# Matmuls of a gated layer listed ahead of their gate operations, and one group's exponentials listed directly behind its logarithms

## Chip, cores and metric

The kernel runs on one core of one Trainium2 chip. The metric is device microseconds (us) of one launch; less is better. TensorE (PE) multiplies matrices, VectorE (DVE) and ScalarE (ACT) work element by element, GpSimd (POOL) and SyncE (SP) issue transfers here. PEld is TensorE's loading of the stationary operand.

## What is computed

The reference has two blocks: a gated recurrence over 768 steps for 4 batches of 8 heads of width 48, and behind it a dense layer with a cosine gate.

```python
mag = np.sqrt(a_re * a_re + a_im * a_im)
scale = np.minimum(mag, 0.999) / (mag + 1e-06)
a_re_n, a_im_n = (a_re * scale, a_im * scale)
for t in range(S):
    new_re = ar * S_re - ai * S_im
    new_im = ar * S_im + ai * S_re
    kv = np.einsum('bhd,bhe->bhde', k[:, :, t], v[:, :, t])
    S_re, S_im = (new_re + kv, new_im)
    y[:, :, t] = np.einsum('bhd,bhde->bhe', q[:, :, t], S_re)
...
h = x @ w_in          # x: 3072 x 384, w_in: 384 x 2048
g = h * np.cos(h)
return (g @ w_out).astype(np.float32)
```

The attention inputs are float32. The two layer weights arrive as float64 and are turned into float32 on the chip.

## The kernel before

The 3072 rows are 24 chunks of 128 steps, worked on in 12 groups of two chunks (G = 2). In place of the recurrence, each chunk uses prefix sums. The logarithm of the decay's size and the angle of the decay are summed along the steps by a matmul with a triangular matrix; keys and queries are multiplied by the exponential of the one sum and the cosine and sine of the other; then a causal product of queries and keys gives the chunk's part, and a carried state the rest. The steps of one group g are:

- `logs(g)`, which calls `g_log`: squares, Ln and Exp on ACT with six DVE operations in between (tiles `lg`, `mag`, `rs`, `tan`), and then the load of the next group's `re` and `im`.
- `p_powers(g, i)`: matmuls of the sums (PSUM tile `lgs`) and two Exp on ACT for each chunk (`P`, in the buffer `lg`, and `Q`).
- `g_angle(g)`: one Arctan on ACT, in place in `tan`. `g_carry(g)` does nothing for groups 0 and 1.
- `p_even` and `p_apply`: three and two DVE operations on P, Q, k and q; `p_even` also issues the transfers `row` and `end` on SP.
- `phases(g)`, which calls `g_phase`: matmuls of the angles (PSUM tile `phs`), a cast on ACT and a subtraction on DVE for each chunk.
- `keys(g)`: `g_trig` (two Sin on ACT, one DVE operation) and `g_stack` (four DVE products, tiles `ks` and `qs`). For group 1, `turned` transposes them on PE (tile `tp`, copied to `kT` and `qT`).
- `chunks(g)`: causal products (`sc`), state (`sp`), output (`yp`), and at the end `f_xt`, which carries the result through memory into `xT`, the layer's input. Group 0 does this in its own way, by `f_rows` and `f_columns`.
- `first(g)`: eight calls of `mm1`. Each multiplies `xT` with one of eight parts of `w_in` into one PSUM bank (`hp`), takes Sin and Square of it on ACT (`gate`, `junk`) and multiplies on DVE (`gate`). `second(g, i)` multiplies the gates with `w_out` (`op`).

The weights come in 16 parts, 0 to 7 of `w_in` (`into`) and 8 to 15 of `w_out` (`back`), through four buffers `raw`. POOL issues the transfer of a part when a buffer is free. `convert` makes floats of a part: a TENSOR_SCALAR, a SCALAR_TENSOR_TENSOR and a CUSTOM_DVE on DVE, and one ACTIVATE on ACT between them (`raw`). The CUSTOM_DVE frees the buffer. The text calls these conversion 0 to 15. The first `RAW` = 4 of them are listed earlier.

The order comes from three things. The program order is a list that `weave` merges from several parts, each spread evenly over a stretch of the list. All matmuls, all table functions of ACT (`special`: Ln, Exp, Sin, Arctan) and all POOL transfers are chained and keep that order on their engine. The other operations of DVE, ACT and SP are set in a fixed order for each engine at build time, by their place in the list and by when the build reckons them ready. On the chip each engine then goes through its queue in order. Ln and Exp are in one table set of ACT and Arctan and Sin in another; `preload` lists a table load (line L699) at each change between them.

PSUM has eight banks: five of the pool `pa` (tag `a`), and three of `pm`, two with the tag `m` and one with the tag `acc`. An `hp` tile keeps its bank until its DVE product has read it.

Around the change the list before is: `logs(1)`, conversion 4, load of group 2's `re` and `im`, conversion 5, tile 0, conversion 6, tile 1, conversion 7, tiles 2 and 3, the two `p_powers(1)`, conversion 8, `g_angle(1)`, `p_even` and `p_apply`, load of group 2's `k` and `q`, tile 4, conversion 9, phase 0, tile 5, phase 1, conversion 10, `g_trig(1)`, tile 6, `g_stack(1)`, conversion 11, tile 7. "Tile" is one `mm1(0, jp)` with its matmuls and gate operations. Then a second `weave` has conversions 12 to 15, `second(0, 0)`, the transposes of group 1, `logs(2)`, `chunks(1)` and `prods(2)`. A third has `second(0, 1)`, `phases(2)`, `keys(2)` and `first(1)`, and from there the groups follow each other alike.

Of the kernel before, what the change touches and what calls it, by code (L numbers as in the profile page):

```python
# [11 lines left out]
F32 = mybir.dt.float32  # L12
# [475 lines left out]
def fast_path(ctx, tc, q, k, v, a_re, a_im, moe_w_in, moe_w_out, out, least, odd, wide):  # L488
# [9 lines left out]
    C = 128  # L498
    NCH = S // C
    G = 2  # L500
# [20 lines left out]
    pa = ctx.enter_context(tc.tile_pool(name="pa", bufs=5, space=PSUM))  # L521
    pm = ctx.enter_context(tc.tile_pool(name="pm", bufs=3, space=PSUM))
# [20 lines left out]
    X = [dict() for _ in range(NG)]  # L543
# [6 lines left out]
    def load(g, names, i=None, put=nc.sync.dma_start):  # L550
        for name in names:
            ap = {"re": a_re, "im": a_im, "q": q, "k": k, "v": v}[name]
            if name not in X[g]:
                X[g][name] = ld.tile([C, G, H, D], F32, tag=name, name=name,
                                     bufs=2 if name == "v" else 1)
            b, c = divmod(g * G + (i or 0), NCH)
            one, n = i or 0, G if i is None else 1
            steps = ap[b].rearrange("h (c p) d -> p c h d", p=C)[:, ds(c, n)]
            tile_ = X[g][name][:, ds(one, n)]
            parts = [(0, C, 0)]  # L560
            if name in ("re", "im") and g >= PEG:

                parts = [(0, C - 16, 1), (C - 16, C - 1, 1)]
                put(out=tile_[C - 1:C], in_=steps[0:1])
            for i_ in range(n):
                for lo, hi, by in parts:
                    put(out=tile_[lo:hi, i_], in_=steps[lo + by:hi + by, i_])
# [18 lines left out]
    RAW = stage["bufs"]  # L586
# [96 lines left out]
    def matmul(out, **kw):  # L683
        chain(nc.tensor.matmul(out, **kw), "tensor")  # L684
# [16 lines left out]
    def special(func, **kw):  # L701
        preload(tables[func])
        chain(nc.scalar.activation(func=func, **kw))  # L703
# [4 lines left out]
    def temp(tag, bufs=1):  # L708
        return gt.tile([C, G * DM], F32, tag=tag, name=tag, bufs=bufs)
# [5 lines left out]
    def cut(t, i, n):  # L715
        return (flat(t) if len(t.shape) == 4 else t)[:, ds(i * DM, n * DM)]
# [59 lines left out]
    def summed_up(ps, g, i, name, ones):  # L776

        if g < PEG:
            matmul(ps, lhsT=ones, rhs=cut(X[g][name], i, 1), start=True, stop=True)
            return  # L780
        chunks_ = range(i + 1) if name == "tan" else [i]
        terms = [(half, c) for half in ("hi", "lo") for c in chunks_]
        for half, c in terms:
            matmul(ps, lhsT=exact if c == i else alls, rhs=cut(X[g][half], c, 1),
                   start=((half, c) == terms[0]), stop=((half, c) == terms[-1]))

    def p_powers(g, i):

        x = X[g]
        if i == 0:  # L790
            x["P"], x["Q"] = x["lg"], temp("Q")
            x["row"] = rows_d.tile([G * DM], F32, tag="row", name="row")
            x["end"] = ft.tile([D2, G * H], F32, tag="end", name="end")
        ps = pa.tile([C, DM], F32, tag="a", name="lgs")
        summed_up(ps, g, i, "lg", sums[0])
        special(out=cut(x["P"], i, 1), in_=ps, func=AF.Exp)
        special(out=cut(x["Q"], i, 1), in_=ps, func=AF.Exp, scale=-1.0)
# [35 lines left out]
    def g_angle(g, i, n):  # L833

        at = cut(X[g]["tan"], i, n)
        special(out=at, in_=at, func=AF.Arctan)
# [172 lines left out]
            out=xt.rearrange("p c g t -> p c (g t)"),  # L1009
            in_=moved.rearrange("p s d t -> (p s d) t").rearrange("(c r) t -> r c t", r=C))  # L1010

    def mm1(g, jp):
        x = X[g]
        third = len(x.setdefault("gate", {})) % 3 == 2
        ps = pm.tile([C, 2, G * C], F32, tag="acc" if third else "m", name="hp",
                     bufs=1 if third else 2)
        for ji in range(2):
            for dc in range(ND):
                matmul(ps[:, ji], lhsT=w_in[:, jp, dc, ts(ji, C)],
                       rhs=x["xT"][:, dc].rearrange("p g t -> p (g t)"),  # L1020
                       start=(dc == 0), stop=(dc == ND - 1))
        gate = msb.tile([C, 2, G * C], F32, tag="gate", name="gate", bufs=8)
        junk = msb.tile([C, 2, G * C], BF16, tag="junk", name="junk", bufs=1)
        special(out=gate, in_=ps, func=AF.Sin, scale=1.0 / in_scale, bias=half_pi_b)
        scalar.activation(out=junk, in_=ps, func=AF.Square, scale=1.0 / in_scale,
                          accum_out=wide[:, ds(g * (NJ // 2) + jp, 1)])
        gated = vector.tensor_tensor(out=gate, in0=ps, in1=gate, op=ALU.mult)
        x.setdefault("gated", gated)
        x["gate"][jp] = gate

    def mm2(g, i, j0, nj):
        if j0 == 0:
# [104 lines left out]
    def weave(*parts):  # L1137

        items = []
        for p, (part, lo, hi) in enumerate(parts):  # L1140
            part = list(part)
            items += [(lo + (hi - lo) * (i + 0.5) / len(part), p, t)
                      for i, t in enumerate(part)]
        for _, _, t in sorted(items, key=lambda x: x[:2]):
            t()
# [4 lines left out]
    def keys(g):  # L1150

        if not 0 <= g < NG:
            return
        for i, n in spans(g):
            yield lambda i=i, n=n: g_trig(g, i, n)
            yield lambda i=i, n=n: (g_stack(g, i, n), p_end(g, i, n))
            for name in "kT", "qT":
                if g >= PEG:
                    yield lambda i=i, n=n, name=name: f_transpose(g, i, n, name)
# [4 lines left out]
    def prods(g):  # L1164
        if not 0 <= g < NG:
            return
        for i in range(G):
            yield lambda i=i: p_powers(g, i)
        yield lambda: g_angle(g, 0, G)
        yield lambda: g_carry(g)  # L1170
        yield lambda: (p_even(g, 0, G), p_apply(g, 0, G))

    def logs(g):
        yield from each(g_log, g)
        if 0 <= g and g + 1 < NG:
            yield lambda: load(g + 1, ("re", "im"))

    def phases(g):
        return [lambda i=i: g_phase(g, i) for i in range(G)] if 0 <= g < NG else []
# [11 lines left out]
    def first(g):  # L1191
        order = range(NJ // 2) if g < PLAIN else (0, 4, 1, 5, 2, 6, 3, 7)
        return [lambda jp=jp: mm1(g, jp) for jp in order]
# [4 lines left out]
    def convert(parts):  # L1198
        return [lambda dst=dst, src=src: weight(dst, src)() for dst, src in parts]
# [12 lines left out]
    into, back = weight_parts()  # L1212
# [35 lines left out]
    for t in (turned(0, 0, "kT") + turned(0, 0, "qT") + early[:1]  # L1248
# [5 lines left out]
              + [lambda: next(one, None), lambda: next(two, None),  # L1254
                             lambda: load(2, ("v",))]):
        t()
    weave((logs(1), 0.0, 0.1), (convert(into[RAW:]), 0.0, 0.5),
          (first(0), 0.2, 1.0), (prods(1), 0.55, 0.58), ([lambda: load(2, ("k", "q"))], 0.58, 0.6),
          (phases(1), 0.7, 0.8), (keys(1), 0.8, 0.9), (convert(back[:4]), 0.5, 1.0))
    over = [t for i in range(G) for name in ("kT", "qT") for t in turned(1, i, name)]  # L1260
    weave((convert(back[4:]), 0.0, 0.3), (second(0, 0), 0.0, 0.65), (over, 0.2, 0.6),
          (logs(2), 0.3, 0.31), (chunks(1), 0.7, 1.0), (prods(2), 0.85, 0.87))
# [89 lines left out]
```

## Time and profile before

| | before |
|---|---|
| median of 3 runs | 677.03 us (676.07 to 678.66) |
| span of the profiled execution | 677.3 us, 0.3 us above that median; the profile gives no other time for that execution |
| busy: PE, PEld, DVE, ACT, POOL | 647.8, 580.3, 490.3, 396.4, 28.5 us |
| ACT table loads | 26, 33.4 us |
| mean granted TensorE clock | 0.985 |

Busy times are of the whole span. The stretch that the change touches is about 48 to 123 us. A row of the timeline has start, duration, engine, line, operation, output <- inputs, shapes, count, and in brackets the idle time before it with what ended it. Line L684 is the helper that lists every matmul, L703 that of ACT's table functions, and L673 that of DVE's and ACT's other operations, so operations are told apart by tile names. A float32 matmul of the program shows as two MATMUL records; a tile `hp` has 12. Matmul rows of one kind are pipelined, so the time from one start to the next is used for their cost, not the printed length of a row.

### The profile page before, as it was taken

The page shows a single profiled execution, that of the slowest core. Times are in us where ns is not written, and L with a number is a line of the kernel's source. Part 1 is how long each engine was busy: PE and PEld are TensorE (multiplying, and loading weights), DVE is VectorE, ACT ScalarE, POOL GpSimd, SP SyncE. Part 2 cuts the span into 40 slices and gives each one's busy share as a digit, 9 for nine tenths or more (in the row PEclk, how much of TensorE's full clock was granted, in tenths as well). Part 3 has the DMA queues.
Part 4 walks back from the last instruction along what each step waited for, and adds up shares of the span by engine and source line. Part 5 has one row for each costly group of instructions (what it writes and reads, how often), then busy time and mean ns, then how long its engine had stood idle before and what let it go on. Part 6 is the DMA issues. An engine that isn't in the chain of part 4 may idle for free.

```text
span 677.3 us, 10771 instructions
## 1 busy us (share of the span) xinstructions
PE 647.8 (96%) x4080; PEld 580.3 (86%) x4080; DVE 490.3 (72%) x792; ACT 396.4 (59%) x730; POOL 28.5 (4%) x47
## 2 busy tenths in 40 slices
PE   5788889999999999999999999999999999999995
PEld 5686657886799999999999999989999989999895
DVE  4879888759868778868768778868768769762251
ACT  5869775475466467367467467467367467432330
POOL 2011100000000000000000000000000000000000
PEclk8979899999999999999999999999999999999998
DMA  9778623923743864764864864854864753363000
GB/s 244 176 234 224 173 72 81 227 66 69 213 92 63 219 137 116 210 142 109 224 140 118 210 140 113 214 113 126 223 145 118 211 138 78 116 139 116 24 6 24
DMA packets 232810, 94.90 MB, mean 140 GB/s; under 512 B 208798, under 2 KB 221217, under 8 KB 232748
## 3 DMA queue, kind: packets, MB, share of 16 engines
q1 hardware_dynamic: 226252, 68.62, 44.5%
q0 software_dynamic: 5632, 25.17, 11.4%
q8 instruction: 34, 0.56, 0.4%
q10 hardware_dynamic: 864, 0.33, 0.2%
q14 instruction: 28, 0.23, 0.1%
HBM read 69.28 MB, written 24.81 MB: 139 GB/s over the span
## 4 chain that ended last, share of the span: by engine, by line
PE 79%; DVE 6%; DMA 6%; ACT 5%; issue 2%; SPq 1%; DVEq 0%; ACTq 0%
PE hp L684 32%; PE sum L684 15%; PE op L684 14%; PE yp L684 5%; PE sc L684 5%; PE sp L684 3%; PE phs L684 2%; DVE w_in L673 1%; PE lgs L684 1%; DMA raw<-in_moe_w_out_dram 1%; DMA xT<-x 1%; DMA qT<-moved 1%; DVE mag L673 1%; PE yr L684 1%; ACT L699 1%
## 5 line engine op out<-in xcount | busy, mean ns | idle before, releaser
L684 PE MATMUL hp<-xT,w_in 128*128 128x256 f32 x1152 | 254.2, 382 | 1.3 <-ACT xT L673 0.6
L684 PEld LDWEIGHTS hp<-xT,w_in 128*128 128x128 f32 x1152 | 219.9, 192 | 34.6 <-DMA xT<-x 1.9
L703 ACT ACTIVATE gate<-hp,half_pi_b 128x512 f32<-128x512 f32 x96 | 65.9, 686 | 128.0 <-PE hp L684 128.0
L673 DVE TENSOR_TENSOR gate<-hp,gate 128x512 f32<-128x512 f32 x96 | 65.5, 683 | 58.4 <-ACT junk L673 58.4
L684 PE MATMUL op<-w_out,gate 128*128 128x192 f32 (+1 forms) x448 | 103.0, 375 | 2.7 <-DVE w_out L673 2.7
L684 PEld LDWEIGHTS op<-w_out,gate 128*128 128x128 f32 x448 | 75.7, 190 | 19.7 <-DVE w_out L673 3.9
L673 ACT ACTIVATE junk<-hp 128x512 bf16<-128x512 f32 x96 | 56.5, 588 | 0.0
L684 PE MATMUL sum<-t_s,s 128*128 128x192 f32 x320 | 55.3, 326 | 0.0
L684 PEld LDWEIGHTS sum<-t_s,s 128*128 128x128 f32 x320 | 52.6, 190 | 0.0
L673 DVE TENSOR_TENSOR atm<-sc,causal 128x512 f32<-128x512 f32 x48 | 33.0, 687 | 25.4 <-PE sc L684 25.2
L684 PEld LDWEIGHTS sc<-qT,kT 96*128 96x128 f32 x384 | 47.6, 192 | 4.2 <-issue 2.2
L684 PE MATMUL sc<-qT,kT 96*128 96x128 f32 x384 | 49.4, 276 | 1.9 <-ACT qT L673 0.9
L673 ACT ACTIVATE ot<-sum 128x192 f32<-128x192 f32 x30 | 9.5, 320 | 49.4 <-PE sum L684 49.4
L699 ACT ACT_TABLE_LOAD x26 | 33.4, 1283 | 4.0 <-DMA ident<-ident_const 3.6
L673 ACT CAST tan<-phs 128x384 int32<-128x384 f32 x24 | 11.5, 479 | 39.7 <-PE phs L684 39.7
L673 DVE SCALAR_TENSOR_TENSOR ot<-op,ot 128x192 f32<-128x192 f32 x31 | 11.0, 354 | 32.3 <-ACT ot L673 23.5
L684 PE MATMUL yp<-atm,v 128*48 128x128 f32 x352 | 33.5, 277 | 0.0
L684 PEld LDWEIGHTS sp<-v,ks 128*96 128x96 f32 x320 | 29.7, 165 | 0.0
L684 PE MATMUL sp<-v,ks 128*96 128x48 f32 x320 | 29.6, 245 | 0.0
L684 PE MATMUL sum<-w_out,gate 128*128 128x192 f32 x160 | 29.6, 329 | 0.0
L684 PE MATMUL yp<-qT,state 96*48 96x128 f32 x304 | 29.6, 272 | 0.0
L684 PE MATMUL op<-t_a,gate 128*128 128x192 f32 x160 | 29.0, 332 | 0.0
(137 smaller groups left out, 992.7 us busy)
## 6 DMA issues: line engine op xcount, KB each, us to landing
moved<-tr SPq DMA_DIRECT2D x20, 768.0 KB
raw<-in_moe_w_in_dram POOLq DMA_DIRECT2D x16, 768.0 KB, 5.5
raw<-in_moe_w_out_dram POOLq DMA_DIRECT2D x16, 768.0 KB, 4.9
kT<-moved SPq DMA_DIRECT2D x40, 192.0 KB
qT<-moved SPq DMA_DIRECT2D x10, 768.0 KB
k<-in_k_dram SPq DMA_DIRECT2D x24, 192.0 KB
q<-in_q_dram SPq DMA_DIRECT2D x24, 192.0 KB
v<-in_v_dram SPq DMA_DIRECT2D x24, 192.0 KB
```

The source lines that it names most:

```text
L673: ins = getattr(self.engine, op)(**kw)
L684: chain(nc.tensor.matmul(out, **kw), "tensor")
L699: chain(nc.scalar.preload_act_table_set(table))
L703: chain(nc.scalar.activation(func=func, **kw))
```

## The change

`mm1` is split in two functions: `mm1_sums` lists the matmuls of a tile, `mm1_gate` its two ACT operations and its DVE product. `mm1` calls one after the other, as before. For group 0, the matmuls of tiles 0 to 3 are listed ahead of any gate operation. Tile 3 of group 0 takes a bank of the pool `pa`, and the turn of the tags `m` and `acc` for tiles 4 to 7 is moved by one.

For group 1, `prods` no longer lists the powers and the angle. They are listed by hand: the powers behind `logs(1)`, conversion 4 and the matmuls of tiles 0 and 1, and the angle behind conversion 5 and the matmuls of tiles 2 and 3. Then come gates 0 and 1, both phases, gates 2 and 3, and conversions 6 and 7. A `weave` of what is left follows: tile 4, conversion 8, `p_even` and `p_apply`, the load of `k` and `q`, tile 5, conversion 9, `g_trig`, `g_stack`, tile 6, conversion 10, tile 7, conversion 11. The second and third `weave` are as before.

```diff
-    def mm1(g, jp):
-        x = X[g]
-        third = len(x.setdefault("gate", {})) % 3 == 2
-        ps = pm.tile([C, 2, G * C], F32, tag="acc" if third else "m", name="hp",
-                     bufs=1 if third else 2)
+    def mm1_sums(g, jp):
+        x = X[g]
+        made = len(x.setdefault("gate", {})) + len(x.setdefault("hp", {}))
+        if g == 0 and jp == 3:
+            ps = pa.tile([C, 2, G * C], F32, tag="a", name="hp")
+        elif (made - (g == 0 and jp > 3)) % 3 == 2:
+            ps = pm.tile([C, 2, G * C], F32, tag="acc", name="hp", bufs=1)
+        else:
+            ps = pm.tile([C, 2, G * C], F32, tag="m", name="hp", bufs=2)
...
+        x["hp"][jp] = ps
+
+    def mm1_gate(g, jp):
+        x = X[g]
+        ps = x["hp"].pop(jp)
...
+    def mm1(g, jp):
+        mm1_sums(g, jp)
+        mm1_gate(g, jp)
...
-        for i in range(G):
-            yield lambda i=i: p_powers(g, i)
-        yield lambda: g_angle(g, 0, G)
+        if g != 1:
+            for i in range(G):
+                yield lambda i=i: p_powers(g, i)
+            yield lambda: g_angle(g, 0, G)
...
-    weave((logs(1), 0.0, 0.1), (convert(into[RAW:]), 0.0, 0.5),
-          (first(0), 0.2, 1.0), (prods(1), 0.55, 0.58), ([lambda: load(2, ("k", "q"))], 0.58, 0.6),
-          (phases(1), 0.7, 0.8), (keys(1), 0.8, 0.9), (convert(back[:4]), 0.5, 1.0))
+    ahead = [lambda jp=jp: mm1_sums(0, jp) for jp in range(4)]
+    gates = [lambda jp=jp: mm1_gate(0, jp) for jp in range(4)]
+    powers = [lambda i=i: p_powers(1, i) for i in range(G)]
+    later = convert(into[RAW:])
+    for t in (list(logs(1)) + later[:1] + ahead[:2] + powers + later[1:2] + ahead[2:]
+              + [lambda: g_angle(1, 0, G)] + gates[:2] + phases(1) + gates[2:] + later[2:]):
+        t()
+    weave((first(0)[4:], 0.0, 1.0), (prods(1), 0.1, 0.2),
+          ([lambda: load(2, ("k", "q"))], 0.3, 0.32),
+          (keys(1), 0.4, 0.6), (convert(back[:4]), 0.0, 1.0))
```

## The prediction

> **What bounds it now.** I read the page's slices first, then a table by stage, then the chain of waits, then PE's and DVE's timelines between 48 and 123 us. The page's slices (a digit is a tenth of 16.9 us) put the loss at the front:
>
> ```profile
> PE   5788889999999999999999999999999999999995
> DVE  4879888759868778868768778868768769762251
> ```
>
> PE has nines from the eighth slice (119 us) on. Behind that point the program is one queue of matmuls, so the change can only pay by letting group 1's layer matmuls (at 122.39 us) start earlier. The table by stage (us, and the number of instructions, for PE, PEld, DVE, ACT, POOL; then the clock):
>
> ```profile
> 49.40:63.60 14.20, 13.87 (x56) 11.25 (x55) 14.18 (x19) 12.68 (x21) 2.38 (x3) 0.89 0.68 187
> 63.60:76.70 13.10, 9.14 (x31) 6.44 (x30) 10.13 (x13) 11.48 (x20) 2.17 (x3) 0.87 0.73 189
> 76.70:96.74 20.04, 17.30 (x79) 12.20 (x79) 19.78 (x30) 13.93 (x22) 1.44 (x2) 1.00 0.46 138
> 96.74:122.39 25.65, 25.20 (x181) 19.02 (x179) 19.51 (x28) 16.44 (x26) 0.00 (x0) 1.00 0.42 88
> ```
>
> Up to 96.74 us DVE is nearly full (14.18 of 14.20 and 19.78 of 20.04 us) except in the second row; from there PE is full. The second row is where the change acts. The chain of waits there:
>
> ```profile
> 64.45 1.28 ACT L699
> ...
> 67.41 1.28 ACT L699
> 68.70 0.85 ACT tan L703
> 69.60 2.93 PE phs L684 x4
> ...
> 95.79 0.95 DVE w_out L673
> 96.74 0.88 DVE lg L673
> ...
> 118.51 3.84 DMA xT<-x
> 122.39 0.70 PE hp L684 x2
> ```
>
> ACT loads the table of Exp, takes the powers, loads the table of Sin back and takes the Arctan; PE stands in front of the angle sums. Later the chain hangs on the last conversion of `w_out` and on group 2's logs behind it. Timelines of PE and DVE:
>
> ```profile
> 69.60 1.65 PE L684 MATMUL phs<-tan,turns 128*128 128x384 f32 x2 [3.96 <-ACT tan L703]
> 87.64 1.56 PE L684 MATMUL op<-w_out,gate 128*128 128x384 f32 x4 [1.47 <-DVE w_out L673]
> 91.19 2.85 PE L684 MATMUL op<-w_out,gate 128*128 128x384 f32 x8 [0.68 <-DVE w_out L673]
> 95.93 2.85 PE L684 MATMUL op<-w_out,gate 128*128 128x384 f32 x8 [0.58 <-DVE w_out L673]
> ...
> 64.47 0.69 DVE L673 TENSOR_TENSOR gate<-hp,gate 128x512 f32<-128x512 f32 x1 [0.89 <-ACT junk L673]
> 76.72 0.69 DVE L673 TENSOR_TENSOR gate<-hp,gate 128x512 f32<-128x512 f32 x1 [2.07 <-ACT junk L673]
> 92.71 0.56 DVE L673 TENSOR_SCALAR w_out<-raw 128x768 uint32<-128x768 uint32 x1 [0.24 <-DMA raw<-in_moe_w_out_dram]
> ```
>
> PE's large wait is 3.96 us. But once past it PE waits for DVE's conversions, 2.73 us in three places. DVE's own idle time from 49.40 to 96.74 us is 0.89 + 2.07 + 0.24 = 3.20 us.
>
> **Table loads.** Logs and powers now share a table, Arctan and gates the other: two loads go, 2 x 1.28 = 2.57 us of ACT. No other instruction is added or removed. The Trainium skill (ScalarE: Activation LUTs, Rules for kernel authors) says to budget about 2.7 us per switch of set, which would make it 5.4 us; all 26 loads here took 1.283 us, so the row is used. ACT is not what is late from 76.7 us on (13.93 of 20.04 us busy), so this saving counts only through PE and DVE.
>
> **PE's queue.** Two tiles `hp` took 5.18 us (76.51 to 81.69), 2.59 each; four sums `lgs` 1.29 (61.59 to 62.88) and four `phs` at most 1.3. The first three tiles took 9.89 us instead of 7.77 for a low clock, 2.1 us that stay. From 48.67: tiles 0 and 1 until 55.9, `lgs` until 57.2, tiles 2 and 3 until 62.4, `phs` until 63.7, tiles 4 to 7 (4 x 2.59) until 74.1 us. Before it was 81.7, so PE gains 7.6: the 3.96 us wait, 1.7 of low clock behind it (four `phs` 2.72 instead of 1.3, tile 5 2.90 instead of 2.59), the rest small waits.
>
> What could stand in the way? The powers can start when the first `lgs` are done, at 56.6; four Exp took 1.5 us (65.75 to 67.26), so the load runs at 58.2 and the Arctan at 59.5 to 60.3, 2.1 us before PE asks for it. Its input `tan` is ready on DVE at 58.24. Gate 0 moves from 55.4 to 60.3: Sin and Square 1.15 us, product 0.6, so its bank is free at 62.1 to 62.7 where tile 4 wants it at 63.7, a margin of 1.0 to 1.6 us. Gates 1 to 3 are wanted 2.6 us apart and take 1.15 each, with two casts of 0.45 between them. I book no wait for PE here. Tile 3's bank in `pa` costs nothing: the five in between are `lgs`, `phs` and itself, each read within 5 us.
>
> **DVE, where the gain shrinks.** DVE has the same operations to do before the last conversion. If all 3.20 us of its idle time go, that conversion ends at 93.5 instead of 96.74; that is the most. New idle time: gate 0's product cannot come before 61.5 us, three later than the last log operation (58.2). Conversions 6 and 7 can fill 3.1 us of it (CUSTOM 0.87, TENSOR_SCALAR 0.47, SCALAR_TENSOR_TENSOR 0.87, CUSTOM 0.87), but they are now listed behind gate 3, and whether DVE's queue has them ahead of gate 0 no view of before shows. Bounds: 0 and 3.3 us of idle. I take 1.0, near the low end, since in the timeline conversions fill holes between log operations wherever their data was there (part 7's transfer was issued at 41.87 us). So 3.2 - 1.0 = 2.2 us earlier.
>
> **POOL and SP.** POOL's transfer of a part goes out 0.56 us after the CUSTOM four parts before (81.09 to 81.65, 87.58 to 88.14) and takes 4.6 us to land. Conversion 15 thus ends at least 7.4 us after conversion 11 (0.56, 4.6, then 0.47, 0.87, 0.95); before it was 9.2. By DVE's work conversion 11 ends near 84 to 85 us, so transfers don't bind. On SP, `row` and `end` go earlier with `p_even`, and the load of `k` and `q` waits for `p_apply` as before; they are ready long before group 2 needs them.
>
> **Behind the last conversion** the stage is the last row of the table: PE is busy 25.20 of 25.65 us, and `xT` landed at 122.35, where PE had just finished its other work. A shift of conversion 15, with the logs of group 2 right behind it on DVE, is passed on whole. 677.3 - 2.2 = 675.1 us for the profiled execution; that lies 0.3 above the median, so 674.8.
>
> **Where the 7.6 us of PE go:** 5.4 of them turn into more waiting for conversions 10 to 15: some 8 us in place of 2.73, in gaps of 2 to 4. After the 3.96 us gap the clock cost 1.7 us; one such loss matters only in the last gap, before conversion 14. The Trainium skill (TensorE: Matmul & The Clock Gate, Why this matters for your kernels) calls only idle gaps over about 3 us harmful, which would leave the shorter gaps free. The trace shows a drop without one: from 42.20 us pairs of `yr` matmuls took 0.43 us apart instead of 0.22, and the last gap had been 0.94 us. I add nothing to the sum, since between 81 and 100 us, with gaps up to 1.47 us, the clock stayed at 1.00, but I keep 1.7 us for the range.
>
> **Rivals.**
> 1. DVE waits in line (slower). If its queue has conversions 6 and 7 behind gate 3's product, as the list has them, it stands from 58.2 until that product ends (60.3 + 4 x 1.15 + 0.9 + 0.6 = 66.4) with 3.3 us of work in 8.2: 4.9 us of idle time against 3.2 removed, 1.7 later; PE's gaps grow with it, and a low clock in the last one adds 1.7. 677.0 + 3.4 = 680.4 us. It decides from 3.2 us of new idle time on. For it: the list. Against it: DVE's filled rows.
> 2. More than the idle time. Group 1's `ks` and `qs` are done some 9 us earlier (PE reaches tile 5 at 69 instead of 75 us), so ACT's squares for group 2 (85.20 now, behind `qs`) are too, and its logs run among the last conversions. The 1.88 us that DVE waited at 99.49 for ACT then goes as well: 3.2 + 1.9 = 5.1, 671.9 us. Against it: the first log operation on DVE is listed behind conversion 15.
> 3. Transfers hold it. If conversion 11 stays at 87.6 behind gate 7 and `g_stack`, conversion 15 can't end before 95.0, and with its neighbours in the queue hardly before 96: 676 to 677 us, no difference.
>
> **Numbers.** Half a per cent, 3.4 us, is about what a measurement of this kernel can tell from no change. Forecast 0.33, within it; rival 3 0.10, within it; rival 2 0.27, faster; rival 1 0.30, with a third of it (no low clock, 678.7) within and 0.21 slower. So faster 0.27, same 0.52, slower 0.21. The range runs from just below rival 2 to just below rival 1's end: 671.6 to 680.0.
>
> **What would show it.** Right: 24 table loads; no wait of PE between tile 0 and tile 7, which ends near 74; more waits `op <- DVE w_out`; last CUSTOM near 94.5; `hp` of group 1 at 120. Wrong: that CUSTOM no earlier than 96 (rival 1 if DVE waits for gates 0 to 3, rival 3 if for `raw`), or the gain passing 3.4 us.

## The result, and the profile after

The change makes no difference that can be measured: 678.29 us (675.29 to 680.22, 20 runs) against 678.24 us (675.91 to 681.83, 20 runs) for the kernel before, a ratio of 0.9998 with a 95% interval of 0.9984 to 1.0012. The profiled execution of after took 678.49 us with a span of 676.6, so about 1.9 us lie around the span. The forecast was 674.8, from a median of 677.03 us in three runs of the kernel before; the 20 runs here have 678.24, so 1.2 of the 3.5 us between forecast and result lie in that base.

In what follows, "stage" is the time from group 0's first `hp` matmul to group 1's first, the stretch the change can act on. It took 73.72 us in the shown profile of before (48.67 to 122.39) and 72.76 in that of after (48.49 to 121.25). The rest of the span from there took 554 to 557 us in every kernel that follows; in two profiles each it was 554.9 and 554.8 us before, 555.4 and 555.3 after. The page's slices and group of table loads:

```profile
PE   5789699999999999999999999999999999999996
DVE  4789987759777878777778877777778769762251
...
L699 ACT ACT_TABLE_LOAD x24 | 30.8, 1283 | 4.0 <-issue 3.6
```

24 loads instead of 26, 2.6 us less, as forecast. PE's slices rise sooner, but a dip is now in the fifth (67.6 to 84.6 us), and DVE is as busy as before (490.3 us). The table by stage for after, with the same borders in the work (columns as before: PE, PEld, DVE, ACT, POOL, clock, DMA share, GB/s):

```profile
49.40:63.60 14.20, 14.20 (x57) 11.21 (x56) 12.89 (x18) 12.85 (x22) 2.37 (x3) 0.92 0.72 208
63.60:76.10 12.50, 11.55 (x51) 9.42 (x50) 11.97 (x17) 9.24 (x19) 1.65 (x2) 1.00 0.53 146
76.10:96.55 20.45, 14.55 (x57) 9.20 (x57) 20.13 (x29) 13.77 (x22) 2.59 (x3) 0.83 0.56 154
96.55:121.25 24.70, 24.46 (x179) 18.80 (x179) 18.78 (x26) 15.82 (x27) 0.00 (x0) 1.00 0.46 96
```

In the first two rows PE has lost its hole. In the third it has a larger one than before: 14.55 us busy of 20.45 at a clock of 0.83, against 17.30 of 20.04 at 1.00. DVE is full in that row in both kernels, and the row ends at 96.55 instead of 96.74 us, in both 48.06 to 48.07 us behind the start of the stage. PE's timeline shows both holes:

```profile
64.76 0.91 PE L684 MATMUL phs<-tan,last 128*128 128x384 f32 x2 [0.88 <-DVE tan L673]
65.51 10.52 PE L684 MATMUL hp<-xT,w_in 128*128 128x256 f32 x48
81.32 5.04 PE L684 MATMUL op<-w_out,gate 128*128 128x384 f32 x8 [5.29 <-DVE gate L673]
...
96.55 1.56 PE L684 MATMUL op<-w_out,gate 128*128 128x384 f32 x4 [0.68 <-DVE w_out L673]
...
121.25 5.02 PE L684 MATMUL hp<-xT,w_in 128*128 128x256 f32 x22 [0.24 <-DMA xT<-x]
```

The 3.96 us wait for the Arctan is gone, and tiles 4 to 7 run in one piece until 76.03 us, 5.7 us earlier than before. Then PE stands for 5.29 us in front of `second(0, 0)`. It isn't waiting for the operands: it waits for a bank. With one tile moved to `pa` and the turn of tags moved by one, tile 6 has the only `acc` bank, which `second(0, 0)` wants for `op`. That bank is free when gate 6's product has read it, and the row names this product's engine; that it is the bank and not an operand is shown below, where the wait goes away with the bank. On DVE (first four rows) and ACT (last two):

```profile
62.04 0.69 DVE L673 TENSOR_TENSOR gate<-hp,gate 128x512 f32<-128x512 f32 x1 [1.30 <-ACT junk L673]
...
80.59 0.68 DVE L673 TENSOR_TENSOR gate<-hp,gate 128x512 f32<-128x512 f32 x1
...
94.67 0.95 DVE L673 TENSOR_TENSOR lg<-lg,tan 128x768 f32<-128x768 f32 x1
95.54 0.95 DVE L673 CUSTOM_DVE_ANT_0 w_out<-raw,w_out 128x1536 uint16<-128x1536 uint16 x1
```
```profile
74.64 1.01 ACT L673 ACTIVATE raw<-raw,carrier_b 128x768 uint32<-128x768 uint32 x1 [2.48 <-DMA raw<-in_moe_w_out_dram]
...
78.00 0.67 ACT L703 ACTIVATE gate<-hp,half_pi_b 128x512 f32<-128x512 f32 x1
```

Gate 6's Sin stands on ACT behind a conversion that waited 2.48 us for its transfer, and behind the Sin of `g_trig`; its product on DVE (80.59) stands behind the four products of `g_stack`. After the wait the clock is low, and eight `op` records took 4.87 us (81.32 to 86.19) instead of 2.58:

```profile
78.00:82.00 4.00, 0.68 (x1) 0.50 (x2) 4.00 (x8) 3.14 (x8) 0.00 (x0) 0.62 1.06 289
82.00:86.00 4.00, 4.00 (x8) 2.15 (x7) 4.00 (x7) 2.98 (x3) 0.83 (x1) 0.53 0.16 34
```

So PE won 5.7 us and gave back 7.6 (5.29 of wait, 2.3 of low clock). What set the end is still DVE, as the experiments below show. The chain of waits:

```profile
87.38 5.06 DMA raw<-in_moe_w_out_dram
...
95.54 0.96 DVE w_out L673
...
96.55 1.56 PE op L684 x4
...
116.87 4.33 DMA xT<-x
...
121.25 2.86 PE hp L684 x12
```

It passes through the last transfer of a part, the last CUSTOM of the conversions, and `xT`, and not through PE's wait. The measure for DVE is therefore an account from group 1's first log operation on DVE to the end of the last CUSTOM: its length is the work in it plus DVE's idle time.

### The profile page after: what moved, and what is told of

Read it like the earlier page. It is cut to its first block, busy times and chain, and to the rows that moved or that the text cites. A ratio compares the mean times of both kernels' runs of the same rounds, so it can differ in the third digit from the quotient of the medians.

```text
span 676.6 us, 10769 instructions
## 1 busy us (share of the span) xinstructions
PE 646.8 (96%) x4080; PEld 579.5 (86%) x4080; DVE 490.3 (72%) x792; ACT 393.8 (58%) x728; POOL 28.3 (4%) x47
## 4 chain that ended last, share of the span: by engine, by line
PE 80%; ACT 6%; DMA 5%; DVE 5%; issue 2%; SPq 0%; DVEq 0%; ACTq 0%
PE hp L684 35%; PE op L684 14%; PE sum L684 14%; PE sc L684 5%; PE yp L684 5%; PE sp L684 3%; DMA raw<-in_moe_w_out_dram 2%; PE phs L684 2%; PE lgs L684 1%; DMA xT<-x 1%; DVE w_out L673 1%; ACT raw L673 1%; DMA x<-yT 1%; DVE w_in L673 1%; ACT L699 1%
## 5 line engine op out<-in xcount | busy, mean ns | idle before, releaser
L684 PE MATMUL op<-w_out,gate 128*128 128x192 f32 (+1 forms) x448 | 105.1, 380 | 6.0 <-DVE gate L673 5.3
```

## Experiments

**Both kernels again.** One profile for each had been compared, so both were profiled a second time, unchanged.

> The kernel before once more, for a second profile: how far does the stage (73.72 us from group 0's first layer matmul to group 1's first) move from one execution to the next? If it moves under 0.5 us, the changed kernel's 72.76 is a gain of 1 us that the times can't resolve; if it moves by 1 us or more, 0.96 us is no gain that one profile can show.

> The changed kernel once more, for a second profile. If the stage is a property of the kernel it is 72.3 to 73.2 us again, with PE's gap of about 5.3 us in front of second(0, 0); if executions differ, it is up to 2 us away, and the difference stands in where the clock was low or in when the weight parts landed.

Each took one run: 676.44 us before, 678.15 after. Times in the table are from group 0's first `hp`.

| | stage | tile 7 ends | last CUSTOM ends | DVE: length = work + idle | from there to group 1's layer |
|---|---|---|---|---|---|
| before, as shown | 73.72 | 33.18 | 48.07 | 47.34 = 44.09 + 3.25 | 25.65 |
| before again | 71.77 | 31.41 | 45.69 | 44.96 = 44.10 + 0.86 | 26.08 |
| after | 72.76 | 27.54 | 48.00 | 47.27 = 45.19 + 2.08 | 24.76 |
| after again | 72.36 | 27.70 | 48.01 | 47.28 = 45.16 + 2.12 | 24.35 |

The unchanged kernel lies 1.95 us apart in this stage, so the 0.96 us between the first profiles of before and after are no gain that can be told; the means of two are 72.75 and 72.56. DVE's work is the same in both of its profiles; its idle time was 3.25 us in one and 0.86 in the other. The windows show the larger part. First the profile the forecast was made from, then the second one of the same kernel:

```profile
66.00:70.00 4.00, 0.40 (x1) 0.41 (x2) 3.94 (x6) 3.97 (x7) 0.72 (x1) 0.94 0.59 197
70.00:74.00 4.00, 4.00 (x11) 2.57 (x11) 4.00 (x6) 2.97 (x7) 0.00 (x0) 0.63 0.49 170
```
```profile
66.00:70.00 4.00, 1.63 (x6) 1.08 (x7) 3.95 (x6) 3.97 (x7) 0.72 (x1) 1.00 0.81 289
70.00:74.00 4.00, 3.68 (x16) 2.65 (x15) 3.57 (x6) 3.82 (x7) 0.49 (x1) 1.00 0.48 82
```

PE's and DVE's rows of the second profile:

```profile
68.37 0.91 PE L684 MATMUL phs<-tan,turns 128*128 128x384 f32 x2 [3.18 <-ACT tan L703]
...
119.93 5.23 PE L684 MATMUL hp<-xT,w_in 128*128 128x256 f32 x23 [0.54 <-DMA xT<-x]
```
```profile
73.85 0.69 DVE L673 TENSOR_TENSOR gate<-hp,gate 128x512 f32<-128x512 f32 x1 [0.43 <-ACT junk L673]
...
92.03 1.82 DVE L673 CUSTOM_DVE_ANT_0 w_out<-raw,w_out 128x1536 uint16<-128x1536 uint16 x2
```

Here PE's wait for the Arctan was 3.18 us instead of 3.96, and the clock stayed at 1.00 behind it instead of 0.63. The `gate` product for which DVE had stood 2.07 us was late by 0.43: 1.64 us less. The other part is 0.72 us in front of the `gate` product before it (0.89 in the first profile, 0.17 in the second), and it lies ahead of the Arctan. It goes with a conversion on ACT. The first profile, then the second:

```profile
62.28 1.04 ACT L673 ACTIVATE raw<-raw,carrier_b 128x768 uint32<-128x768 uint32 x1 [1.49 <-DVE w_in L673]
```
```profile
59.91 2.16 ACT L673 ACTIVATE raw<-raw,carrier_b 128x768 uint32<-128x768 uint32 x2
```

The later of the two in the second row began at 61.03, as its part had landed (54.34 + 6.60 us in the chain of waits). Counted from the start of the stage, the conversion came 0.74 us later in the first profile (13.61 against 12.87), and the gate, the table loads and the Arctan behind it on ACT came later with it; so PE's wait was 3.96 us instead of 3.18. A later transfer is the likely reason, but the first row names DVE, so that is not shown. Of the 3.25 us of idle time that the change was to remove, 2.4 belonged to that one execution: 1.64 stood behind the low clock and 0.72 behind the late conversion.

**Holding the clock in the kernel before.** If the low clock makes the 2.07 us, the kernel before must get the short wait there whenever PE is kept busy in front of the Arctan's matmuls. Ten dummy matmuls are listed ahead of `phases(1)`:

```diff
-          (phases(1), 0.7, 0.8), (keys(1), 0.8, 0.9), (convert(back[:4]), 0.5, 1.0))
+          ([lambda: busy(10)], 0.7, 0.71),
+          (phases(1), 0.7, 0.8), (keys(1), 0.8, 0.9), (convert(back[:4]), 0.5, 1.0))
```

> The kernel before with ten matmuls without use (128x128, about 3 us) in front of the first phase matmuls, where PE waits 3.2 to 4.0 us for the Arctan; all else is the same. Theory clock (the two profiles of before differ by whether the clock falls in that wait): the clock stays at 1.00 behind 56 us, DVE's idle time from its first log operation to the last CUSTOM is 0.8 to 1.5 us, the stage (group 0's first layer matmul to group 1's first) 71.3 to 72.2 us. The time may be up to 1 us below before, which 12 runs hardly resolve. If the clock is not the cause, the stage is 72.5 us or more at a clock of 1.00.

> e13 once more, for a second profile. Theory clock: the stage is 71.3 to 72.2 us again. If the stage differs from e13's by over 0.8 us with the clock at 1.00 in both, something else than the clock moves it.

```profile
65.33 2.39 PE L684 MATMUL busy<-sums,ident 128*128 128x128 f32 x20
68.91 0.91 PE L684 MATMUL phs<-tan,turns 128*128 128x384 f32 x2 [1.18 <-ACT tan L703]
```
```profile
66.00:70.00 4.00, 2.82 (x20) 2.23 (x19) 3.94 (x5) 3.97 (x8) 0.72 (x1) 1.00 0.71 258
70.00:74.00 4.00, 3.70 (x16) 2.64 (x14) 3.97 (x6) 4.00 (x7) 0.00 (x0) 1.00 0.48 113
```

The clock stayed at 1.00, DVE's idle time was 1.08 and 1.14 us in the two profiles, and the last CUSTOM ended at 45.92 and 45.99. The stage took 71.35 and 72.24; of the 0.9 between them, 0.71 is a wait for `xT` at its end. That also meets the condition set for the second run: over 0.8 us apart at a clock of 1.00, so something besides the clock moves the stage too. The product that had stood 2.07 us stood 0.42 in both, so in three profiles at a clock of 1.00 it is 0.42 or 0.43. The product before it, ahead of the dummies, stood 0.34 and 0.49. The time was 677.15 us against 677.23 for the kernel before beside it, ratio 1.0003 (0.9989 to 1.0017), and 676.60 in the single run: a microsecond or two is too little for this measurement.

**The bank and the transfers, one at a time.** The first kernel gives `acc` to tile 5 as the old turn would, which takes the bank wait away; the second gives the weights a fifth buffer, so that transfers start earlier.

```diff
-        elif (made - (g == 0 and jp > 3)) % 3 == 2:      # bank freed
+        elif made % 3 == 2:
...
-"bufs": 4}                                              # five buffers
+"bufs": 5}
-RAW = stage["bufs"]
+RAW = 4
```

> As the changed kernel, but tiles 4 to 7 take their banks in the old turn, so tile 5 and not tile 6 has the bank acc, which second(0, 0) takes next. DVE's queue is the same as in the changed kernel. Theory DVE (the conversions' work on DVE sets the end of the stage): PE's wait of 5.29 us for gate 6 turns into waits for conversions 10 and 11; the last CUSTOM of w_out stays at 96 to 97 us, from group 0's first layer matmul to group 1's first it stays 72.8 us (72.76 in the changed kernel, 73.72 before), and the time stays within 0.2% of the changed kernel. Theory bank (the wait for the bank and the low clock behind it, 5.3 + 2.3 us, are what ate the gain): those two starts stand 69 to 71 us apart, and the time is 2 to 4 us below before.

> As the changed kernel, but five raw buffers in place of four, so each transfer of a weight part goes out one conversion earlier; DVE's queue is the same. Theory DVE: DVE loses only its short waits for landed parts, and ACT its 2.48 us wait for raw at 74.6; the last CUSTOM comes at 95 to 96.5 us and group 1's layer starts 72 to 73 us after group 0's, time within 0.25% of the changed kernel. Theory transfers (the last parts land too late): the last part lands 3 to 5 us earlier, the last CUSTOM comes at 92 to 94 us, the two starts are 69.5 to 71 us apart, and the time is 2 to 4 us below before.

```profile
76.35 2.78 PE L684 MATMUL op<-w_out,gate 128*128 128x384 f32 x8
...
85.12 5.33 PE L684 MATMUL op<-w_out,gate 128*128 128x384 f32 x8 [4.25 <-DVE w_out L673]
...
121.23 5.13 PE L684 MATMUL hp<-xT,w_in 128*128 128x256 f32 x23
```

Without the bank wait `second(0, 0)` starts 5 us earlier, runs two parts, and then waits 4.25 us for the conversions. The stage is 72.76 us, that of after to the hundredth; 677.87 us, ratio 0.9992 (0.9973 to 1.0012). The 5.29 us wait is hidden altogether. With five buffers the last transfer goes out at 84.69 instead of 87.38 us, from the start of the stage 36.94 instead of 38.89, 1.95 earlier; but the last CUSTOM ends only 0.2 earlier (47.81) and the stage takes 72.17; 677.56 us, 0.9997 (0.9978 to 1.0015). That part landed at 89.43, and DVE came to it at 91.54 without a wait in front. The transfer that the chain names was not what held conversion 15: DVE's queue was.

**Without the conversions of `w_out`.** Where nobody waits for these conversions, PE's gain must show. The first pair is each kernel without their transfers and conversions, with a constant in `w_out`, so that this part of the computation is missing; the third is after with the bank freed too:

```diff
+    chain(nc.gpsimd.memset(w_out, 0.01), "gpsimd")
...
-convert(back[:4])   convert(back[4:])
+[]                  []
```

> The kernel before with the transfers and conversions of w_out left out: POOL fills w_out once with a constant, so this part of the computation is missing. Some 17.6 us of DVE work and eight transfers are gone. PE's 4 us wait for the angle stays, its 2.7 us of waits for conversions go. Group 1's layer should start 66 to 70 us after group 0's (73.72 before), and the time be 4 to 8 us below before. Both theories say the same here; it is the base for the next run.

> The changed kernel with the transfers and conversions of w_out left out in the same way. Theory DVE: with the cover gone, what the change gives PE (tile 7 ends 5.7 us earlier, 76.03 against 81.69 us) is passed on: group 1's layer starts 4 to 6 us sooner after group 0's than in the run without w_out of the kernel before, and the time is 4 to 6 us below that run's. Theory that PE's gain is no gain (the bank and the order on ACT take it back by themselves): the two runs without w_out differ by under 1.5 us.

> e4 (the changed kernel without transfers and conversions of w_out, so that part of the computation is missing) with the freed bank of e1. Stage 65.85 us in e4 and 67.97 in e3. If the wait of 1.27 us in front of second(0, 0) in e4 is for gate 6's bank, and nothing else holds PE there, the stage is 64.3 to 64.9 us. If the bank isn't the cause, it stays at 65.5 to 66.

The stage starts 5.5 us later in all three (54.15), which goes with the fill on POOL, 5.24 us long; so they are compared with each other. Stages: 67.97 before, 65.85 after, 64.58 after with the bank freed. PE's timelines, of after and then with the bank freed:

```profile
83.62 2.82 PE L684 MATMUL op<-w_out,gate 128*128 128x384 f32 x8 [1.27 <-DVE least L673]
```
```profile
82.45 2.74 PE L684 MATMUL op<-w_out,gate 128*128 128x384 f32 x8
...
118.74 5.56 PE L684 MATMUL hp<-xT,w_in 128*128 128x256 f32 x25
```

Times against the kernel before, complete: 0.9999 (0.9978 to 1.0019), 0.9979 (0.9960 to 0.9998) and 0.9943 (0.9925 to 0.9961). Removing the conversions alone brought nothing, since the stage of before is 5.75 us shorter and starts 5.5 us later; with them gone in both kernels, the change with its bank freed is worth 3.4 us of stage and about 3.8 us of time. So where nobody waits for these conversions, what PE gains reaches the end. The bank wait, which cost nothing with the conversions in place, costs 1.27 us here; its row names `least`, but it goes with the bank. The expectation for after, 4 to 6 us off the stage, was not met: 2.1 us lies between its two theories. PE's own gain is smaller here: tile 7 ends 31.84 us behind the start of the stage before and 28.45 after with the bank freed, the same 3.4 us as the stage.

**Conversions earlier.** On top of the freed bank, the conversions left for later are listed among gates and phases, so that the last transfers go out early.

```diff
-              + [lambda: g_angle(1, 0, G)] + gates[:2] + phases(1) + gates[2:] + later[2:]):
+              + [lambda: g_angle(1, 0, G)] + convert(back[:2]) + gates[:2] + phases(1) + gates[2:]):
...
-          (keys(1), 0.4, 0.6), (convert(back[:4]), 0.0, 1.0))
+          (keys(1), 0.4, 0.6), (convert(back[2:4]), 0.0, 0.3))
```

`later[1:2]` becomes `later[1:]` as well.

> As e1 (the freed bank), and conversions 6 to 11 are listed earlier: 6 and 7 behind the powers, 8 and 9 behind the Arctan, 10 and 11 among tiles 4 and 5. Stage means the time from group 0's first layer matmul to group 1's first; it was 73.72 us before, 72.76 in the changed kernel and in e1. Theory DVE (the sum of DVE's work is the floor): an earlier part only pushes gates, ks and qs later; DVE's idle time falls by up to 1.3 us (the wait for gate 0 is filled), so the stage is 71 to 72.5 us. Theory order (the change lost its gain because conversions 8 to 10 slid behind the gates and keys, and with them the last transfers): the last part lands 5 us earlier, at 86 to 88, the last CUSTOM at 93 to 94 us, and the stage is 69.5 to 71 us.

```profile
67.24 0.91 PE L684 MATMUL phs<-tan,last 128*128 128x384 f32 x2 [4.07 <-DVE tan L673]
```

The last transfer went out at 79.82, from the start of the stage 32.27, 6.6 us earlier than in after, and the last CUSTOM ended at 46.68, 1.3 earlier: 44.04 of work and 1.92 of idle time. But `phases(1)` now stood behind conversions on DVE, PE waited 4.07 us for it, and the stage was 72.51; 677.75 us, 0.9987 (0.9967 to 1.0006). Neither DVE's work nor its idle time fell to what a gain would have needed. It is the lowest ratio of a complete kernel, and not told apart from 1.

**A lighter DVE.** If DVE's work before conversion 15 is the limit, taking work off it must show in both kernels. The SCALAR_TENSOR_TENSOR of the conversions of `w_out` is left out, so the sign bits of `w_out` are missing; the second kernel is after with the bank freed. One line more in the kernel moves the helpers to L674, L685 and L704.

```diff
-        vector.scalar_tensor_tensor(out=bits, in0=hi, scalar=0xC0000000, in1=bits, ...)
+        if dst.shape[-1] != DM:
+            vector.scalar_tensor_tensor(out=bits, in0=hi, scalar=0xC0000000, in1=bits, ...)
```

> The kernel before, with the SCALAR_TENSOR_TENSOR of conversions 8 to 15 left out (the sign bits of w_out are missing); all transfers stay. 8 x 0.87 = 7.0 us of DVE work are gone. Theory DVE: the last CUSTOM comes 3 to 7 us earlier than at 96.74 and the stage is 68 to 71 us (73.72 before). Theory transfers: the last part still lands near 91 to 93 us, and the stage is 72 to 73.5 us.

> e1 (the changed kernel with the freed bank) with the SCALAR_TENSOR_TENSOR of conversions 8 to 15 left out (the sign bits of w_out are missing); all transfers stay. Theory DVE: with 7.0 us less on DVE, more of PE's gain comes through: the stage is 66.5 to 69 us, 2 to 3.5 us shorter than in e7. Theory transfers: the four buffers hold it, the last part lands at 89 us or later, and the stage is 71 to 72.5 us, within 1.2 us of e7.

> e7 once more. Its profiled execution (677.01 us) lay 2.65 us below the median of its runs (679.66), so its stage of 70.18 us may not be the usual one. If executions differ inside the stage, it is 71.5 to 73.5 us here; if the theory of transfers is right as e7 and e8 stood, it is 70 to 70.6 again.

> e8 once more. Its profiled execution had a span of 677.3 us where its median of 677.1 us goes with a span near 675.3. Theory DVE: its stage of 72.28 us was a slow one, and it is 69.5 to 71 us here, below e7's usual one, as the medians have it (677.1 against 679.66). Theory transfers: 72 us or more again.

Times are from group 0's first `hp` again; the last transfer goes out at 39.47 in before and 38.89 in after.

| light | stage | tile 7 ends | last CUSTOM ends | DVE: work + idle | last transfer goes out |
|---|---|---|---|---|---|
| before | 70.18 | 32.32 | 41.31 | 38.05 + 2.54 | 30.51 |
| before again | 72.23 | 34.28 | 43.27 | 38.12 + 4.42 | 32.47 |
| after, bank freed | 72.28 | 29.01 | 46.60 | 39.77 + 6.11 | 37.65 |
| after, bank freed, again | 71.28 | 27.87 | 45.60 | 39.83 + 5.04 | 36.25 |

DVE's work fell by 6.0 us before and by 5.4 after (45.17 to 39.8; two more of group 2's log operations now stand ahead of the last CUSTOM). Before, the mean of the last CUSTOM's ends came 4.6 us earlier (46.88 to 42.29), and the mean stage 1.5 us (72.75 to 71.2). After, it came only 2.3 earlier (48.41 to 46.10), and the stage 1.0 (72.76 to 71.8): idle time took the place of most of the work, first for gate 0's product and later for parts. Two rows of DVE in the first profile of the light after:

```profile
62.88 0.69 DVE L674 TENSOR_TENSOR gate<-hp,gate 128x512 f32<-128x512 f32 x1 [2.78 <-ACT junk L674]
...
91.69 0.56 DVE L674 TENSOR_SCALAR w_out<-raw 128x768 uint32<-128x768 uint32 x1 [1.21 <-DMA raw<-in_moe_w_out_dram]
```

So DVE's work is not the only limit, and the expectations of a stage of 66.5 to 69 us, then of 69.5 to 71, failed. In the order of after, gates and keys stand ahead of conversions 8 to 10 on DVE, and the last transfer still goes out at 36 to 38 us, where in before it came forward to 30.5 to 32.5. The waits for transfers that then show (1.21 and 0.44 us in the first profile) are smaller than those for gates, so that the transfers are the new limit is argued and not shown. The times, with 677.10 us at 0.9974 (0.9957 to 0.9991) for after and 679.66 at 1.0009 (0.9993 to 1.0025) for before, differ in favour of after by 2.6 us, and the four stages don't show that. In before the rest of the span took 556.6 and 557.4 us, some 2 us more than in the complete kernel, so the shorter stage did not reach the time; in after it took 557.2 and 555.6. Why stays open.

**Work moved from DVE to POOL.** The opposite of leaving it out: `p_apply(1)`'s two products, and in the second kernel two of `g_stack`'s as well, run on POOL, with the bank freed and five buffers.

```diff
+        eng = nc.gpsimd if g == 1 else vector     # p_apply
...
+        (nc.gpsimd if g == 1 and name == "qs" else vector)   # g_stack, second kernel alone
```

> The changed kernel with the freed bank of e1, the five buffers of e2, and the two products of p_apply of group 1 on POOL in place of DVE: 1.7 us of DVE work less, nothing left out. From DVE's first log operation of group 1 to the last CUSTOM it took 47.3 us in the changed kernel, 2.1 of it idle. Theory DVE's work: 45.0 to 46.0 us here, the stage (group 0's first layer matmul to group 1's first) 70.5 to 71.7 us against 72.4 to 72.8, and the time 1 to 2 us below e1's and e2's. Theory order: ks and qs wait for POOL's slower products, the conversions keep their places, and the stage stays at 72 to 73 us.

> e9 and the two products qs of group 1's g_stack on POOL too: 3.5 us of DVE work less than in the changed kernel, nothing left out. Theory DVE's work: 43.3 to 44.7 us from the first log operation to the last CUSTOM, the stage 69 to 70.7 us, the time 2.5 to 4 us below before. Theory order: POOL takes the last transfers in line behind qs, so the last part lands later than in e9, and the stage is 71.5 us or more.

They took 678.88 us, 1.0012 (0.9996 to 1.0028), and 679.10 us, 1.0018 (1.0000 to 1.0035); stages 74.79 and 74.27, last CUSTOM at 48.73 and 49.86. The first stage is longer than either theory had; the second fits the theory of order, 71.5 us or more. DVE's work in the account did not fall: 45.21 and 46.52 us. DVE and POOL in the first kernel, then POOL in the second:

```profile
75.06 1.98 DVE L673 CUSTOM_DVE_ANT_0 w_out<-raw,w_out 128x1536 uint16<-128x1536 uint16 x1
76.96 2.15 DVE L673 TENSOR_SCALAR rs<-tan 128x768 uint32<-128x768 uint32 x1
```
```profile
73.81 2.41 POOL L831 TENSOR_TENSOR Q<-k,Q 128x768 f32<-128x768 f32 x1 [2.93 <-DVE Q L673]
76.19 2.51 POOL L832 TENSOR_TENSOR mag<-q,lg 128x768 f32<-128x768 f32 x1
```
```profile
78.88 7.67 POOL L887 TENSOR_TENSOR qs<-mag,rs 128x768 f32<-128x768 f32 x1 [1.14 <-issue]
```

A product that takes DVE 0.95 us took POOL 2.41 to 7.67 by the profile, whose times for POOL are rough. In the first kernel what DVE did meanwhile was stretched: a CUSTOM of 0.95 to 1.98, a TENSOR_SCALAR of 0.56 to 2.15; the second kernel has the same two figures beside its first products. Beside the 7.67 us one DVE's operations kept their usual lengths until 85.40.

**Parts of the change alone.** Only two tiles ahead of their gates, on the old turn of banks; and the four tiles ahead with the powers and angle of group 1 behind the four gates. The lists are shortened here:

```diff
+    logs(1) + later[:1] + ahead[:2] + powers + later[1:2] + [g_angle] + gates[:2]       # two ahead
+        + ahead[2:3] + gates[2:3] + later[2:3] + ahead[3:] + gates[3:] + phases(1) + later[3:]
...
+    logs(1) + later[:2] + ahead + gates[:2] + later[2:3] + gates[2:] + later[3:]        # ahead only
+    weave((first(0)[4:], 0.15, 1.0), (prods(1), 0.0, 0.05), (load(2), 0.06, 0.08),
+          (phases(1), 0.3, 0.5), (keys(1), 0.5, 0.75), (convert(back[:4]), 0.03, 1.0))
```

> The change with the matmuls of only two tiles ahead of the gates; tiles 2 and 3 follow gates 1 and 2, banks in the old turn; powers and angle as in the change, so 24 table loads. PE has to wait for gate 0's bank before tile 3, about 2 us, and ends tile 7 some 30 us after its start (27.5 in the changed kernel, 31.4 to 33.2 before). Theory DVE's work: that doesn't matter, idle time on DVE is 1.5 to 3 us, the stage 72 to 73.5 us and the time within 0.25% of the changed kernel's. If PE's early tiles mattered, the stage would be 1.5 us or more above the changed kernel's.

> The other part alone: the matmuls of four tiles ahead of the gates, but powers and angle of group 1 behind the four gates, so 26 table loads as before. PE waits for the Arctan in front of the phases as before, 2 to 4 us, though with gates 0 to 3 done early DVE gets their products at 55 to 59 us and idles little there. Theory DVE's work: idle time on DVE 1 to 3 us, stage 71.5 to 73.5 us, time within 0.25% of before. If the two table loads were what counts, the stage would be 1.3 us or more above the changed kernel's, 74 us.

679.21 us, 1.0009 (0.9989 to 1.0028), and 678.64 us, 1.0014 (0.9995 to 1.0032), with stages of 74.89 and 75.95. Neither time is told apart from that of before. But both stages are longer than expected (72 to 73.5 and 71.5 to 73.5) and 2 us or more above after's 72.4 to 72.8, which the expectations had set as the sign that PE's early tiles, and the two table loads or what goes with them, do matter. Each is one profiled execution. PE in the first, then in the second:

```profile
63.50 4.54 PE L684 MATMUL hp<-xT,w_in 128*128 128x256 f32 x12 [3.40 <-DVE gate L673]
```
```profile
86.15 4.54 PE L684 MATMUL op<-w_out,gate 128*128 128x384 f32 x8 [2.59 <-DVE gate L673]
```

Two tiles ahead leave the third waiting for gate 0's bank; all four without the powers leave PE waiting for the Arctan (2.58), for the angle's product (3.70) and for a gate. DVE's idle time is 4.78 and 3.63 us, against 2.1 in after. So each half alone leaves DVE waiting longer, and only both together let PE's queue run through.

## Why the prediction was wrong

**Two loads less:** right, 24 loads, 2.6 us.

**PE's queue:** the mechanism was right, the size of one term was not. The forecast let tile 7 end at 74.1; it ended at 76.03. It read four `phs` records as the whole and booked 1.3 us, but that is one chunk; both chunks are listed ahead of tile 4 now, and from 61.78 to 65.51 they took 3.73: twice 1.3, 0.88 of wait for `tan` from DVE, and the rest in small steps. Tiles 2 and 3 ended 0.6 earlier than booked. So PE gained 5.7 us and not 7.6.

**No wait of PE, banks cost nothing:** the tiles 0 to 3 that it looked at behaved so. It followed the banks of `hp` and not the turn of `acc`, which `second(0, 0)` shares. That wait of 5.29 us, the largest of after's stage, was not foreseen. Freeing it changed nothing (72.76 against 72.76 us), so this omission isn't why the time was missed. The forecast let 5.4 us of PE's gain turn into waiting for conversions; with the bank freed, 4.25 us of such a wait stand at one place.

**The step that failed is DVE's: "3.2 - 1.0 = 2.2 us earlier".** Both terms were off, and so was a third that it put at nothing, that DVE has the same operations to do before the last conversion.

- The 3.20 us to remove were one execution's. A second profile of the same kernel had 0.86, and with the clock held 1.08 and 1.14. The forecast took the 2.07 us before a `gate` product for a property of the order; 1.64 of them were the low clock behind a 3.96 us wait, which comes and goes, and 0.72 of the 0.89 us before the product ahead of it went with a conversion on ACT that came later in that execution.
- The new idle time was 2.08 and 2.12 us, not 1.0: 1.30 and 1.47 in front of gate 0's product, as named, and the rest at `tan`, gates and parts. That lies within the bounds given, 0 to 3.3.
- One operation more stood in front of the last CUSTOM, group 2's first log addition at 94.67. It is the only operation that the account has more; work rose from 44.1 to 45.2 us, of which its 0.87 is most.

Together the last CUSTOM came 0.07 us earlier than in the first profile of before (48.00 against 48.07 from the start of the stage) and 2.3 later than in the second.

**"Passed on whole":** nearly. From the last CUSTOM to group 1's layer it took 24.76 and 24.35 us, 0.9 to 1.7 less than before, where that log addition still has to be done. The nine profiles of other complete kernels say nearly the same: with the addition ahead of the last CUSTOM it took 24.35 to 24.41 us in four, with it behind 25.4 to 26.3 in another four; only the kernel with just the four tiles ahead, with 26.72, doesn't fit. So what the operation cost ahead of the CUSTOM was found again behind it. With it, the stage of after (72.4 to 72.8) falls between the two of before (71.8 and 73.7).

**The rivals.** Rival 1 had the right place, DVE in front of gate 0, at about a quarter of its size (1.30 of 4.9 us): conversion 6's CUSTOM and the first two operations of conversion 7 did run ahead of gate 0's product (57.98, 58.84 and 59.78 in DVE's timeline of after), so DVE didn't stand there until 66.4. New idle time stayed under the 3.2 us from which it decides. Rival 2, group 2's logs among the last conversions, did happen with one operation, but as a swap and not as a gain; of the 1.88 us that DVE waited behind it, 1.01 were left. Rival 3 gave the right total of no difference; transfers were in the chain, but five buffers moved the last one 1.95 us and the stage 0.2 to 0.6. Between DVE's work and the transfers there is little room, as the light kernels show, and how much of the limit is the one and how much the other is not settled.

**The idle gap and the clock:** the forecast weighed the Trainium skill's rule of about 3 us (TensorE: Matmul & The Clock Gate, Why this matters for your kernels). The kernel before lies near that length: its wait of 3.96 us was followed by a clock of 0.63 and its wait of 3.18 by 1.00. But two gaps of one length in the light kernel after had different outcomes (last section), so here the length of the gap alone doesn't settle it. The forecast's 1.7 us was in the right place and priced for PE; that the low clock had also made half of DVE's idle time was not seen.

## What to carry to other kernels

Before booking a stall as gain, profile the kernel before a second time: a wait that lies behind a long PE gap may be a draw of that one execution and not a property of the order. Count the limiting engine's work up to the instruction that sets the end, and its idle time apart from it; a reordering that frees another engine is worth only what it takes from this account. Follow each PSUM tag to its next user in another stage when tiles change their turn.

## What had not been expected of the hardware

- A gap of 3.18 us in PE's work left the clock at 1.00; 3.96 us brought it to 0.63, and the same kernel had both. That went with most of a difference of 2 us in this stage from one execution to another. In the first profile of the light kernel before, 3.06 us were enough; PE's row, and then the window behind it with a clock of 0.50:

```profile
68.47 0.91 PE L685 MATMUL phs<-tan,turns 128*128 128x384 f32 x2 [3.06 <-ACT tan L704]
```
```profile
70.00:72.00 2.00, 2.00 (x6) 1.65 (x5) 2.00 (x4) 2.00 (x4) 0.00 (x0) 0.50 0.87 263
```

- The same gap in the same kernel had both outcomes: in the two profiles of the light after, 2.91 us left the clock at 1.00 (82 to 90 us), and 2.92 were followed by 0.50 (82 to 84 us). The first profile, then the second:

```profile
83.19 1.56 PE L685 MATMUL op<-w_out,gate 128*128 128x384 f32 x4 [2.91 <-DVE w_out L674]
```
```profile
81.09 4.54 PE L685 MATMUL op<-w_out,gate 128*128 128x384 f32 x8 [2.92 <-DVE w_out L674]
```

- POOL beside DVE can cost twice: 2.41 to 7.67 us for a product of 128 x 768 floats that takes DVE 0.95, and DVE's own instructions up to 3.8 times longer (0.56 to 2.15 us). The Trainium skill (GPSIMD Engine Reference, Specifications) says that POOL's SBUF interfaces are shared with VectorE, with contention for VectorE's instructions in a two-port mode or with two SBUF inputs; these rows agree with a contention and put a price on it in a running kernel.
